# Value products ahead of the next head's scores, w4 in four pieces and a result of four rows, in a decoding attention block

## The chip, the cores and the metric

The kernel runs on one core of a Trainium2 chip. The metric is the device time of one execution in microseconds. A core has engines with queues of their own: TensorE (PE; its weight loads are listed as PEld) multiplies matrices, VectorE (DVE) and ScalarE (ACT) work on elements, GpSimd (POOL) makes a small constant here, and SyncE (SP) issues nearly all loads. Sixteen DMA engines move the data.

## The reference

One token (x, 512 numbers) goes through attention over a cache of 16384 positions and then through a small MLP. There are 32 query heads and 8 key/value heads of 128; four query heads share a key/value head. LN is a layer normalization without weights.

```python
def A(x):                                   # x: LN of the input
    q = (x @ wq) as 32 heads of 128
    scores = q . k_cache * 128 ** -0.5      # 16384 positions, 8 heads of K
    p = softmax(scores)
    return (p . v_cache) @ wo               # 4096 -> 512

def B(x):                                   # x: LN of h
    h = gelu(LN(x) @ w1)
    x1 = x + concat(four shifted quarters of h) @ w2
    return x1 + gelu(LN(x1) @ w3) @ w4      # 512 -> 1792 -> 512

h  = x + A(LN(x))
h2 = h + B(LN(h))
```

With a sequence of one position, each shifted quarter is the padding, that is zero. So the term with w1 and w2 vanishes, x1 is LN(h), and the kernel never loads w1 and w2.

## The kernel before

The kernel is written for each engine as a list of instructions with explicit semaphores (class `Program`). `P.op(engine, ...)` appends an instruction with the tokens that it waits for, and `P.dma("sp", ...)` a load. Each engine works through its list in order, so the order of the calls in the Python text is the order on each engine; engines meet only through tokens. A wait at the head of a list holds back all that stands behind it on that engine.

**Loads.** SP issues all loads but that of x. For a head g these are two halves of K (2 MB each, `kraw`, three buffers), wo(g) (0.5 MB, two buffers), and four pieces of V (1 MB each, six slots: two of their own, `vown`, and four in the place of wq once it has been used, `wq_sb`). A load waits until its buffer has been read: half n of K for the transpose of half n - 3, piece n of V for the products of piece n - 6, wo(g) for project(g - 2). The names k_free, v_free and wo_free hold these tokens. w3 and w4 (1.8 MB each) come last and wait for nothing but their place in SP's list.

**One head.** VectorE transposes K blockwise from `kraw` to `kt`, half by half (`transpose_half`, L226). `scores(g)` (L252) is 128 products on TensorE with kt as weights, `softmax_exp(g)` (L260) four exponentials on ScalarE that also sum up, `denominators(g)` (L266) one fp32 product that adds the sums over partitions, `reciprocal_den(g)` (L284) and `normalize(g)` (L287) two small steps on VectorE. `values(g)` (L276) is 128 products with V as weights, 32 for each piece, and `project(g)` (L296) 16 products with wo that add onto one column of results, `h_ps`. `h_ps` starts with x itself (L305).

**The loop (L309 to L331).** In round g TensorE's list gets scores(g+1), denominators(g), project(g-1), values(g), in this order. VectorE's list gets the two transposes of g+1 with reciprocal_den(g-1) between them, then normalize(g-1). SP's list gets K(g+1), wo(g), V(g). The last round has no K.

**The tail (L332 to L383).** After project(7) two layer normalizations are made in one (L340 to L356), which gives `xc`, the input of the MLP, and `xsum`, all that is added to the MLP's result. Then 56 products with w3 as weights (L366), two Gelus into `hcol` (L370), and 56 products with w4 as weights (L376), whose result is a column layout, 128 partitions by 4; the first waits for all of w4. One add (L381) makes `fin`, and the output is written from 128 partitions, 4 numbers each.

Of the kernel before, what the change touches and what calls it, by code (L numbers as in the profile page):

```python
# [6 lines left out]
FP32 = mybir.dt.float32  # L7
BF16 = mybir.dt.bfloat16
ALU = mybir.AluOpType
# [3 lines left out]
D = 512  # L13
HQ = 32
G = 8
# [4 lines left out]
NCH = D // 128  # L20
NHC = FM // 128
# [4 lines left out]
QTR = NJ * DH  # L26
NKR = 3
NVS = 6
SCALE = 1.0 / math.sqrt(DH)
EPS = 1e-5  # L30

# [50 lines left out]
def bass_sequential_preLN__gqa_block_cached__mixer_s_mlp__decode_kernel(  # L82
# [14 lines left out]
    with ctx:  # L97
        sb = lambda name, shape, dt: ctx.enter_context(nc.sbuf_tensor(name, shape, dt))
        ps = lambda name, shape, dt: ctx.enter_context(nc.psum_tensor(name, shape, dt))
        P = Program(lambda name: ctx.enter_context(nc.semaphore(name)))  # L100
# [7 lines left out]
        xc = sb("xc", [128, NCH], BF16)  # L108
        x1 = sb("x1", [128, NCH], FP32)
        xsum = sb("xsum", [128, NCH], FP32)  # L110
        fin = sb("fin", [128, NCH], BF16)
        mean_f = sb("mean_f", [128, 128], FP32)
        ones_f = sb("ones_f", [128, 128], FP32)
        ident = sb("ident", [128, 128], BF16)
        sel = sb("sel", [128, 4, 128], BF16)
        mask = sb("mask", [128, NQ], FP32)
# [7 lines left out]
        hcol = sb("hcol", [128, NHC], BF16)  # L124
        wo_sb = [sb(f"wo_sb{i}", [128, REP, D], BF16) for i in range(2)]
        w3_sb = sb("w3_sb", [128, NCH, FM], BF16)
        w4_sb = sb("w4_sb", [128, NHC, D], BF16)
# [7 lines left out]
        ot_ps = [ps(f"ot_ps{i}", [128, 512], FP32) for i in range(2)]  # L135
# [6 lines left out]
        w4_in = B_w4.rearrange("(m d) c -> d m c", d=128)  # L142
# [7 lines left out]
        for a in range(NQ):  # L150
            t_mask = P.op("dve", lambda e, a=a: e.memset(mask[32 * a:32 * a + 32, a:a + 1], 1.0), t_m0)
        t_scr = P.op("dve", lambda e: e.memset(scr[:, :], 1.0))
        t_id = P.op("pool", lambda e: e.affine_select(
            out=ident[:, :], in_=ident[:, :], pattern=[[-1, 128]], compare_op=ALU.not_equal,
            fill=1.0, base=0, channel_multiplier=1), t_id0)

        t_sel = None
        for be in range(4):
# [12 lines left out]
        def load_k(g, hf):  # L171
            n = 2 * g + hf
            src = A_k_cache[0, g].rearrange("(p j) d -> p (j d)", p=128)[:, hf * HALF:(hf + 1) * HALF]
            k_land[n] = P.dma("sp", kraw[n % NKR][:, :], src, k_free.get(n - NKR))
# [14 lines left out]
        def stats(src, ln, st, waits, sq_scale=1.0):  # L189
# [9 lines left out]
        t = stats(xcol[:, :], ln1, st1, [t_x])  # L199
        t = P.op("dve", lambda e: e.tensor_scalar(st1[:, 2:3], st1[:, 0:1], st1[:, 0:1], EPS,  # L200
                                                  ALU.mult, ALU.subtract), t)
# [4 lines left out]
        t = P.op("dve", lambda e: e.reciprocal(st1[:, 4:5], st1[:, 3:4]), t)  # L206
# [13 lines left out]
        def transpose_half(g, hf):  # L220
            n = 2 * g + hf
            src = bass.AP(kraw[n % NKR][:, :].bitcast(FP32).tensor, 0,
                          [[HALF // 2, 128], [HALF // 4, 2], [32, 2 * NJ], [1, 32]])
            dst = bass.AP(kt[g % 2][:, :].bitcast(FP32).tensor, 2 * hf,
                          [[HALF, 128], [1, 2], [128, 2 * NJ], [4, 32]])
            k_free[n] = P.op("dve", lambda e: e.transpose(dst, src), k_land[n], t_qk.get(g - 2))  # L226
            return k_free[n]
# [15 lines left out]
        def scores(g):  # L243
            for J in range(NJ):
                for be in range(4):
                    b, e_ = divmod(be, 2)
                    o = J * 512 + b * 256 + e_
                    lhs = bass.AP(kt[g % 2], o, [[2 * HALF, 128], [2, 128]])
                    rhs = Qbd[:, (be * G + g) * 16:(be * G + g + 1) * 16]
                    last = J == NJ - 1 and be == 3  # L250
                    waits = (t_qbd, t_kt[g], t_exp.get(g - 2)) if J == 0 and be == 0 else ()
                    t = P.op("pe", lambda e, J=J, l=lhs, r=rhs, be=be: e.matmul(  # L252
                        s_ps[g % 2][:, 16 * J:16 * J + 16], l, r, start=(be == 0), stop=(be == 3)),
                        *waits, sig=last)
            t_qk[g] = t

        def softmax_exp(g):
            src = s_ps[g % 2][:, :].rearrange("p (t h) -> p h t", h=REP)
            for h in range(REP):
                t_exp[g] = P.op("act", lambda e, h=h: e.activation(  # L260
                    p_sb[g % 2][:, h * 128:(h + 1) * 128], src[:, h, :], ACTF.Exp, scale=float(SCALE),
                    accum_out=accden[g % 2][:, h:h + 1]),
                    *((t_qk[g], t_pv.get(g - 2), t_den.get(g - 2)) if h == 0 else ()), sig=(h == REP - 1))

        def denominators(g):
            t_den[g] = P.op("pe", lambda e: e.matmul(  # L266
                den_ps[:, 0:REP], ones_f[:, :], accden[g % 2][:, :], start=True, stop=True),
                t_exp[g], t_ones, t_rden.get(g - 1))

        def values(g):  # L270
            pv = p_sb[g % 2][:, :].rearrange("p (h t) -> p t h", h=REP)
            for a in range(NQ):
                n = NQ * g + a
                for J in range(NJ):
                    waits = (v_land[n], t_exp[g], t_norm.get(g - 2)) if J == 0 else ()
                    t = P.op("pe", lambda e, J=J, a=a, n=n: e.matmul(  # L276
                        ot_ps[g % 2][:, 0:REP], vslot[n % NVS][:, J * DH:(J + 1) * DH],
                        pv[:, J * NQ + a, :], start=(a == 0 and J == 0),
                        stop=(a == NQ - 1 and J == NJ - 1)), *waits, sig=(J == NJ - 1))
                v_free[n] = t  # L280
            t_pv[g] = t

        def reciprocal_den(g):
            t_rden[g] = P.op("dve", lambda e: e.reciprocal(rden[g % 2][:, :], den_ps[:, 0:REP]), t_den[g])  # L284

        def normalize(g):
            t_norm[g] = P.op("dve", lambda e: e.tensor_tensor(  # L287
                OT[g % 2][:, :], ot_ps[g % 2][:, 0:REP], rden[g % 2][:, :], ALU.mult),
                t_pv[g], t_rden[g], wo_free.get(g - 2))

        def project(g):
            for h in range(REP):
                for k in range(NCH):
                    last = h == REP - 1 and k == NCH - 1
                    lhs = bass.AP(wo_sb[g % 2], h * D + k, [[REP * D, 128], [NCH, 128]])
                    t = P.op("pe", lambda e, h=h, k=k, l=lhs: e.matmul(  # L296
                        h_ps[:, k:k + 1], l, OT[g % 2][:, h:h + 1], start=False,
                        stop=(g == G - 1 and h == REP - 1), skip_group_check=True),
                        *((t_norm[g], wo_land[g]) if h == 0 and k == 0 else ()), sig=last)
            wo_free[g] = t  # L300
# [7 lines left out]
        softmax_exp(0)  # L308
        for g in range(G):  # L309
            if g + 1 < G:  # L310
                for hf in range(2):
                    load_k(g + 1, hf)
                    t_kt[g + 1] = transpose_half(g + 1, hf)
                    if g >= 1 and hf == 0:
                        reciprocal_den(g - 1)
            elif g >= 1:
                reciprocal_den(g - 1)
            load_wo(g)
            for a in range(NQ):
                load_v(g, a)  # L320
                if a == 0:
                    if g >= 1:
                        normalize(g - 1)
                    if g + 1 < G:
                        scores(g + 1)
                        softmax_exp(g + 1)
                    denominators(g)
                    if g >= 1:
                        project(g - 1)
                    pass  # L330
            values(g)  # L331
        t_w3 = P.dma("sp", w3_sb[:, :, :], w3_in)  # L332
        t_w4 = P.dma("sp", w4_sb[:, :, :], w4_in)
        reciprocal_den(G - 1)
        normalize(G - 1)
        project(G - 1)


        P.op("act", lambda e: e.activation(scr[:, 3:4], scr[:, 0:1], ACTF.Sqrt), sig=False)
# [20 lines left out]
        cut = NHC // 2  # L360
        parts = [(0, cut), (cut, NHC)]
        t_h = []
        for i, (m0, m1) in enumerate(parts):
            for m in range(m0, m1):
# [4 lines left out]
                        *((t_xc, t_w3) if m == 0 and k == 0 else ()), sig=(m == m1 - 1 and k == NCH - 1))  # L369
            t_h.append(P.op("act", lambda e, i=i, m0=m0, m1=m1: e.activation(  # L370
                hcol[:, m0:m1], s_ps[i][:, 0:m1 - m0], ACTF.Gelu_apprx_tanh), t))
        for i, (m0, m1) in enumerate(parts):
            for m in range(m0, m1):
                for k in range(NCH):
                    lhs = bass.AP(w4_sb, m * D + k, [[NHC * D, 128], [NCH, 128]])
                    t = P.op("pe", lambda e, m=m, k=k, l=lhs: e.matmul(  # L376
                        ot_ps[0][:, k:k + 1], l, hcol[:, m:m + 1], start=(m == 0 and k == 0),
                        stop=(m == NHC - 1), skip_group_check=True),
                        *((t_h[i], t_w4) if m == m0 and k == 0 else ()),
                        sig=(m == NHC - 1 and k == NCH - 1))  # L380
        t = P.op("dve", lambda e: e.tensor_tensor(fin[:, :], xsum[:, :], ot_ps[0][:, 0:NCH], ALU.add), t, t_sum)  # L381
        t = P.dma("sp", out[0, 0, :].rearrange("(p k) -> p k", k=NCH), fin[:, :], t)
        P.wait("sp", t)  # L383

        block = ctx.enter_context(nc.Block())
# [50 lines left out]
```

## Time and profile before

| | |
|---|---|
| median of three runs | 209.55 us (209.37 to 209.74) |
| the profiled execution | 209.99 us |
| its span (first to last instruction) | 208.1 us |
| DMA: bytes, mean rate | 79.50 MB, 382 GB/s |
| chain that ended last: DMA, DVE, PE, issue | 43%, 25%, 15%, 14% |

The span is 1.9 us shorter than the time of the same execution; the rest lies around it. Rows of the timeline and of the stretches give times in us from the start of the span. In a group's row stand the line, the engine, the operation, what is written and read, the shapes, the count, and after the first bar the busy time and the mean duration of one in ns; after the second bar stands the engine's idle time before them and what ended it. In a row of a stretch stand its bounds and length, the busy time of PE, PEld, DVE, ACT and POOL, the granted clock of TensorE, the busy share of the DMA engines, and GB/s.

### The profile page before, as it was taken

The page shows a single profiled execution, that of the slowest core. Times are in us where ns is not written, and L with a number is a line of the kernel's source. Part 1 is how long each engine was busy: PE and PEld are TensorE (multiplying, and loading weights), DVE is VectorE, ACT ScalarE, POOL GpSimd, SP SyncE. Part 2 cuts the span into 40 slices and gives each one's busy share as a digit, 9 for nine tenths or more (in the row PEclk, how much of TensorE's full clock was granted, in tenths as well). Part 3 has the DMA queues.
Part 4 walks back from the last instruction along what each step waited for, and adds up shares of the span by engine and source line. Part 5 has one row for each costly group of instructions (what it writes and reads, how often), then busy time and mean ns, then how long its engine had stood idle before and what let it go on. Part 6 is the DMA issues. An engine that isn't in the chain of part 4 may idle for free.

```text
span 208.1 us, 5140 instructions
## 1 busy us (share of the span) xinstructions
PE 74.0 (36%) x2441; PEld 72.0 (35%) x2441; DVE 123.4 (59%) x64; ACT 16.1 (8%) x77; POOL 0.5 (0%) x5
## 2 busy tenths in 40 slices
PE   0105115038204730373027500960086107913532
PEld 0005114038204730373027500960086107913432
DVE  2194799963995299519970799069915992100300
ACT  2120002002000200020002000200010000400210
POOL 0000000000000000000000000000000000000000
DMA  6999999999999999999999999999999992699950
GB/s 243 463 403 419 431 422 392 417 431 431 383 416 439 422 389 420 431 422 394 414 436 425 393 415 438 416 404 409 425 441 379 408 402 83 231 411 432 371 175 3
DMA packets 13541, 79.50 MB, mean 382 GB/s; under 512 B 1232, under 2 KB 7120, under 8 KB 7120
## 3 DMA queue, kind: packets, MB, share of 16 engines
q1 hardware_dynamic: 13376, 79.17, 93.1%
q8 instruction: 19, 0.31, 0.6%
q10 hardware_dynamic: 144, 0.00, 0.0%
q14 instruction: 2, 0.02, 0.0%
HBM read 79.17 MB, written 0.00 MB: 380 GB/s over the span
## 4 chain that ended last, share of the span: by engine, by line
DMA 43%; DVE 25%; PE 15%; issue 14%; SPq 1%; ACT 0%
DMA kraw<-in_A_k_cache_dram 29%; DVE kt L226 23%; DMA w_sb<-in_B_w_dram 10%; PE s_ps L252 7%; DMA xcol<-in_A_x_dram 4%; PE ot_ps L276 3%; PE ot_ps L215 2%; SPq L58 1%; PE ot_ps L376 1%; PE den_ps L266 1%; PE h_ps L296 1%; DVE Qbd L238 0%; PE den_ps L193 0%; DVE OT L287 0%; PE ot_ps L234 0%
## 5 line engine op out<-in xcount | busy, mean ns | idle before, releaser
L226 DVE STREAM_TRANSPOSE kt<-kraw 128x4096 f32<-128x4096 f32 x16 | 117.6, 7407 | 40.0 <-DMA kraw<-in_A_k_cache_dram 40.0
L252 PE MATMUL s_ps<-Qbd,kt 128*128 128x16 bf16 x1024 | 28.6, 174 | 87.6 <-DVE OT L287 68.4
L252 PEld LDWEIGHTS s_ps<-Qbd,kt 128*128 128x128 bf16 x1024 | 27.9, 104 | 88.2 <-DVE OT L287 68.9
L276 PE MATMUL ot_ps<-p_sb,wq_sb 128*128 128x4 bf16 x640 | 19.0, 168 | 10.8 <-issue 5.9
L276 PEld LDWEIGHTS ot_ps<-p_sb,wq_sb 128*128 128x128 bf16 x640 | 18.1, 103 | 11.3 <-issue 6.3
L260 ACT ACTIVATE p_sb<-s_ps 128x128 bf16<-128x128 f32 x32 | 8.4, 277 | 157.0 <-PE s_ps L252 157.0
L276 PE MATMUL ot_ps<-p_sb,vown 128*128 128x4 bf16 x384 | 11.6, 168 | 6.6 <-issue 3.7
L276 PEld LDWEIGHTS ot_ps<-p_sb,vown 128*128 128x128 bf16 x384 | 11.1, 104 | 6.9 <-issue 3.8
L287 DVE TENSOR_TENSOR OT<-ot_ps,rden 128x4 bf16<-128x4 f32 x8 | 1.3, 157 | 15.9 <-PE ot_ps L276 15.9
L296 PEld LDWEIGHTS h_ps<-OT,wo_sb 128*128 128x128 bf16 x128 | 6.0, 125 | 2.5 <-issue 2.1
L215 PE MATMUL ot_ps<-xn,wq_sb 128*128 128x1 bf16 x128 | 3.6, 165 | 8.6 <-DVE kt L226 8.6
L260 ACT ACTIVATION_READ_ACCUMULATOR p_sb<-s_ps 128x1 f32 x32 | 6.6, 207 | 0.0
L215 PEld LDWEIGHTS ot_ps<-xn,wq_sb 128*128 128x128 bf16 x128 | 3.5, 104 | 8.7 <-DVE kt L226 8.7
L296 PE MATMUL h_ps<-OT,wo_sb 128*128 128x1 bf16 x128 | 5.5, 172 | 2.3 <-issue 2.1
L266 PE MATMUL den_ps<-accden,ones_f 128*128 128x4 f32 x16 | 4.5, 354 | 0.0
L193 PE MATMUL den_ps<-ln,mean_f 128*128 128x8 f32 x4 | 1.2, 371 | 9.2 <-DVE ln L191 9.2
L193 PEld LDWEIGHTS den_ps<-ln,mean_f 128*128 128x128 f32 x4 | 1.0, 312 | 9.3 <-DVE ln L191 9.3
L381 DVE TENSOR_TENSOR fin<-xsum,ot_ps 128x4 bf16<-128x4 f32 x1 | 0.2, 157 | 6.7 <-PE ot_ps L376 6.7
L266 PEld LDWEIGHTS den_ps<-accden,ones_f 128*128 128x128 f32 x16 | 4.0, 311 | 0.0
L284 DVE RECIPROCAL rden<-den_ps 128x4 f32<-128x4 f32 x8 | 1.3, 163 | 4.4 <-PE den_ps L266 4.4
L190 DVE CAST ln<-xcol 128x4 f32<-128x4 bf16 x1 | 0.2, 171 | 6.0 <-DMA xcol<-in_A_x_dram 6.0
L376 PE MATMUL ot_ps<-hcol,w_sb 128*128 128x1 bf16 x56 | 2.0, 172 | 3.5 <-DMA w_sb<-in_B_w_dram 3.5
(46 smaller groups left out, 19.0 us busy)
## 6 DMA issues: line engine op xcount, KB each, us to landing
kraw<-in_A_k_cache_dram SPq DMA_DIRECT2D x16, 2048.0 KB, 19.6
wq_sb<-in_A_v_cache_dram SPq DMA_DIRECT2D x20, 1024.0 KB, 13.5
vown<-in_A_v_cache_dram SPq DMA_DIRECT2D x12, 1024.0 KB, 13.8
wq_sb<-in_A_wq_dram SPq DMA_DIRECT2D x1, 4096.0 KB, 16.7
wo_sb<-in_A_wo_dram SPq DMA_DIRECT2D x8, 512.0 KB, 8.4
w_sb<-in_B_w_dram SPq DMA_DIRECT2D x2, 1792.0 KB, 19.4
xcol<-in_A_x_dram ACTq DMA_DIRECT2D x1, 1.0 KB, 7.6
out_dram<-fin SPq DMA_DIRECT2D x1, 1.0 KB, 3.1
```

Source lines behind the costliest of these rows:

```text
L58: self.lists[engine].append((waits, lambda e: e.dma_start(out, in_), (sem, 16)))
L193: t = P.op("pe", lambda e: e.matmul(den_ps[:, 0:2 * NCH], mean_f[:, :], ln[:, :], start=True, stop=True), t, t_mean)
L215: t_q = P.op("pe", lambda e, h=h, k=k: e.matmul(ot_ps[0][:, h:h + 1], wq_sb[:, k, h * DH:(h + 1) * DH], xn[:, k:k + 1], start=(k == 0), st ...
L226: k_free[n] = P.op("dve", lambda e: e.transpose(dst, src), k_land[n], t_qk.get(g - 2))
L252: t = P.op("pe", lambda e, J=J, l=lhs, r=rhs, be=be: e.matmul(s_ps[g % 2][:, 16 * J:16 * J + 16], l, r, start=(be == 0), stop=(be == 3)), ...
L260: t_exp[g] = P.op("act", lambda e, h=h: e.activation(p_sb[g % 2][:, h * 128:(h + 1) * 128], src[:, h, :], ACTF.Exp, scale=float(SCALE), ac ...
L266: t_den[g] = P.op("pe", lambda e: e.matmul(den_ps[:, 0:REP], ones_f[:, :], accden[g % 2][:, :], start=True, stop=True), t_exp[g], t_ones, ...
L276: t = P.op("pe", lambda e, J=J, a=a, n=n: e.matmul(ot_ps[g % 2][:, 0:REP], vslot[n % NVS][:, J * DH:(J + 1) * DH], pv[:, J * NQ + a, :], s ...
L284: t_rden[g] = P.op("dve", lambda e: e.reciprocal(rden[g % 2][:, :], den_ps[:, 0:REP]), t_den[g])
L287: t_norm[g] = P.op("dve", lambda e: e.tensor_tensor(OT[g % 2][:, :], ot_ps[g % 2][:, 0:REP], rden[g % 2][:, :], ALU.mult), t_pv[g], t_rden ...
L296: t = P.op("pe", lambda e, h=h, k=k, l=lhs: e.matmul(h_ps[:, k:k + 1], l, OT[g % 2][:, h:h + 1], start=False, stop=(g == G - 1 and h == RE ...
L376: t = P.op("pe", lambda e, m=m, k=k, l=lhs: e.matmul(ot_ps[0][:, k:k + 1], l, hcol[:, m:m + 1], start=(m == 0 and k == 0), stop=(m == NHC ...
```

## The change

It has three parts.

1. The loop is put in another order. SP's list stays as it was. On TensorE a round is now denominators(g), values(g), scores(g+1), project(g); on VectorE both transposes of g+1, reciprocal_den(g), normalize(g). The three steps for head 7 that stood behind the loop are in its last round.
2. w4 is loaded by four DMAs of 5, 4, 3 and 2 of its 14 blocks, each with a semaphore of its own.
3. The products with w4 are turned around. `hcol` (one column) is the weight and 128 columns of w4 are streamed, so the result is four rows of 128, on partitions 0, 32, 64 and 96. `xsum` is brought into the same rows by 16 fp32 products with an identity (`ident_f`, made by VectorE at the start), onto a tile that VectorE has set to zero. The result is copied (128 by 128) to `fin` and written from four partitions, 128 numbers each.

```diff
+W4_CUTS = [(0, 5), (5, 9), (9, 12), (12, 14)]
...
-        fin = sb("fin", [128, NCH], BF16)
+        fin = sb("fin", [128, 128], BF16)
...
+        t_idf = P.op("dve", lambda e: e.tensor_copy(ident_f[:, :], ident[:, :]), t_id)
...
             if g + 1 < G:
-                for hf in range(2):
-                    load_k(g + 1, hf)
-                    t_kt[g + 1] = transpose_half(g + 1, hf)
-                    if g >= 1 and hf == 0:
-                        reciprocal_den(g - 1)
-            elif g >= 1:
-                reciprocal_den(g - 1)
+                load_k(g + 1, 0)
+                load_k(g + 1, 1)
             load_wo(g)
             for a in range(NQ):
                 load_v(g, a)
-                if a == 0:
-                    if g >= 1:
-                        normalize(g - 1)
-                    if g + 1 < G:
-                        scores(g + 1)
-                        softmax_exp(g + 1)
-                    denominators(g)
-                    if g >= 1:
-                        project(g - 1)
-                    pass
+            denominators(g)
+            if g + 1 < G:
+                transpose_half(g + 1, 0)
+                t_kt[g + 1] = transpose_half(g + 1, 1)
+            reciprocal_den(g)
             values(g)
+            normalize(g)
+            if g + 1 < G:
+                scores(g + 1)
+                softmax_exp(g + 1)
+            project(g)
         t_w3 = P.dma("sp", w3_sb[:, :, :], w3_in)
-        t_w4 = P.dma("sp", w4_sb[:, :, :], w4_in)
-        reciprocal_den(G - 1)
-        normalize(G - 1)
-        project(G - 1)
+        t_w4 = [P.dma("sp", w4_sb[:, m0:m1, :], w4_in[:, m0:m1, :]) for m0, m1 in W4_CUTS]
...
-        for i, (m0, m1) in enumerate(parts):
+        t_row = P.op("dve", lambda e: e.memset(ot_ps[0][:, 0:128], 0.0), t_norm[G - 2])
+
+        row_ps = ot_ps[0]
+        for q in range(4):
+            for k in range(NCH):
+                P.op("pe", lambda e, q=q, k=k: e.matmul(
+                    bass.AP(row_ps, 32 * q * 512 + k, [[512, 1], [NCH, 32]]), xsum[:, k:k + 1],
+                    ident_f[:, 32 * q:32 * q + 32], start=(k == 0), stop=False, skip_group_check=True),
+                    *((t_sum, t_idf, t_row) if q == 0 and k == 0 else ()), sig=False)
+        for (m0, m1), t_w in zip(W4_CUTS, t_w4):
             for m in range(m0, m1):
-                for k in range(NCH):
-                    lhs = bass.AP(w4_sb, m * D + k, [[NHC * D, 128], [NCH, 128]])
-                    t = P.op("pe", lambda e, m=m, k=k, l=lhs: e.matmul(
-                        ot_ps[0][:, k:k + 1], l, hcol[:, m:m + 1], start=(m == 0 and k == 0),
-                        stop=(m == NHC - 1), skip_group_check=True),
-                        *((t_h[i], t_w4) if m == m0 and k == 0 else ()),
-                        sig=(m == NHC - 1 and k == NCH - 1))
-        t = P.op("dve", lambda e: e.tensor_tensor(fin[:, :], xsum[:, :], ot_ps[0][:, 0:NCH], ALU.add), t, t_sum)
-        t = P.dma("sp", out[0, 0, :].rearrange("(p k) -> p k", k=NCH), fin[:, :], t)
+                for q in range(4):
+                    waits = (t_w, t_h[int(m >= cut)]) if q == 0 and m in (m0, cut) else ()
+                    t = P.op("pe", lambda e, m=m, q=q: e.matmul(
+                        row_ps[32 * q:32 * q + 1, 0:128], hcol[:, m:m + 1], w4_sb[:, m, 128 * q:128 * (q + 1)],
+                        start=False, stop=(m == NHC - 1), skip_group_check=True),
+                        *waits, sig=(m == NHC - 1 and q == 3))
+        t = P.op("dve", lambda e: e.tensor_copy(fin[:, :], row_ps[:, 0:128]), t)
+        t = P.dma("sp", out[0, 0, :].rearrange("(q c) -> q c", q=4), bass.AP(fin, 0, [[32 * 128, 4], [1, 128]]), t)
```

More of the change, by code (lines that the diff above doesn't have):

```diff
@@ L110, in bass_sequential_preLN__gqa_block_cached__mixer_s_mlp__decode_kernel @@
         xsum = sb("xsum", [128, NCH], FP32)
-        fin = sb("fin", [128, NCH], BF16)
+        fin = sb("fin", [128, 128], BF16)
         mean_f = sb("mean_f", [128, 128], FP32)
         ones_f = sb("ones_f", [128, 128], FP32)
+        ident_f = sb("ident_f", [128, 128], FP32)
         ident = sb("ident", [128, 128], BF16)
```

## The prediction

> **What bounds the kernel now.** I read the page from the top: the engines' shares, the slices, then the queues.
>
> ```profile
> PE 74.0 (36%) x2441; PEld 72.0 (35%) x2441; DVE 123.4 (59%) x64; ACT 16.1 (8%) x77; POOL 0.5 (0%) x5
> GB/s 243 463 403 419 431 422 392 417 431 431 383 416 439 422 389 420 431 422 394 414 436 425 393 415 438 416 404 409 425 441 379 408 402 83 231 411 432 371 175 3
> ...
> q1 hardware_dynamic: 13376, 79.17, 93.1%
> q8 instruction: 19, 0.31, 0.6%
> ```
>
> No engine that computes is above 59%, and the data queue is busy for 93.1% of 16 engines. The kernel is a stream of 79.17 MB. It runs at about 400 GB/s in every slice but the first, the last two, and slices 34 and 35 (83 and 231). Next I asked for the stretches around those two slices.
>
> ```profile
> 20.00:171.00 151.00, 53.53 (x1818) 52.28 (x1815) 109.03 (x28) 8.00 (x56) 0.00 (x0) 1.00 1.01 416
> 171.00:180.00 9.00, 6.97 (x243) 6.97 (x244) 2.16 (x3) 2.63 (x10) 0.00 (x0) 1.00 0.31 110
> 171.00:172.00 1.00, 0.00 (x0) 0.00 (x0) 1.00 (x1) 0.00 (x0) 0.00 (x0) 1.00 0.68 279
> 173.00:174.00 1.00, 0.97 (x36) 0.97 (x37) 0.00 (x0) 0.00 (x0) 0.00 (x0) 1.00 0.39 164
> 174.00:175.00 1.00, 1.00 (x44) 1.00 (x41) 0.00 (x0) 0.00 (x0) 0.00 (x0) 1.00 0.00 0
> 178.00:179.00 1.00, 1.00 (x44) 1.00 (x42) 0.00 (x0) 1.00 (x1) 0.00 (x0) 1.00 0.31 23
> ```
>
> The last two columns are the DMA engines' busy share and GB/s. For 151 us the stream is full at 416 GB/s. From 171 to 180 us it moves 110. From 171 to 174 some of the 16 engines have run out and others (a share of 0.39 in the last of these three) still work; nothing moves at 174, and 0.31 of the engines are back at 178 to 179. The timeline names the cause.
>
> ```profile
> 172.82 0.17 DVE L287 TENSOR_TENSOR OT<-ot_ps,rden 128x4 bf16<-128x4 f32 x1
> 173.03 3.58 PE L252 MATMUL s_ps<-Qbd,kt 128*128 128x16 bf16 x128 [9.23 <-DVE OT L287]
> 176.90 0.67 PE L296 MATMUL h_ps<-OT,wo_sb 128*128 128x1 bf16 x16
> 177.59 0.38 SPq L58 DMA_DIRECT2D wo_sb<-in_A_wo_dram  x1
> 178.01 0.98 SPq L58 DMA_DIRECT2D wq_sb<-in_A_v_cache_dram  x2
> 180.06 0.94 SPq L58 DMA_DIRECT2D w_sb<-in_B_w_dram  x2
> ```
>
> The queue SP issues the load of wo(7) only when project(5) (L296) has read the same buffer. In TensorE's order project(5) stands behind scores(7), and those wait for the last transposes. V(7), w3 and w4 stand behind wo(7) on SP. In earlier heads the same wait is covered by K already queued; for head 7 there is no next K.
>
> The end hangs on that stream:
>
> ```profile
> 192.76 1.02 PE L276 MATMUL ot_ps<-p_sb,vown 128*128 128x4 bf16 x32 [1.48 <-DMA vown<-in_A_v_cache_dram]
> 197.25 1.63 PE L366 MATMUL s_ps<-xc,w_sb 128*128 128x1 bf16 x56 [1.47 <-DVE st L353]
> 198.91 0.18 ACT L370 ACTIVATE hcol<-s_ps 128x7 bf16<-128x7 f32 x1 [0.57 <-PE s_ps L366]
> 202.37 2.00 PE L376 MATMUL ot_ps<-hcol,w_sb 128*128 128x1 bf16 x56 [3.50 <-DMA w_sb<-in_B_w_dram]
> 204.41 0.16 DVE L381 TENSOR_TENSOR fin<-xsum,ot_ps 128x4 bf16<-128x4 f32 x1 [6.74 <-PE ot_ps L376]
> 204.59 0.35 SPq L58 DMA_DIRECT2D out_dram<-fin  x1
> 180.56 21.67 DMA w_sb<-in_B_w_dram
> out_dram<-fin SPq DMA_DIRECT2D x1, 1.0 KB, 3.1
> ```
>
> The last V piece lands at 192.76; hcol is ready at 199.1; w4 lands at 180.56 + 21.67 = 202.2; 56 products, one add and the output follow.
>
> **The change part by part.** *Order in the loop.* TensorE now does den(g), values(g), scores(g+1), project(g); VectorE both transposes of g+1, then the reciprocal and the normalization of g. No instruction is added. SP's order of loads stays; only what it waits for comes earlier. project(5) now follows the products of V(5,3), the load directly ahead of K(7), so wo(7) can be issued most of a head early. V(7,2) and V(7,3) wait for values(6,0) and values(6,1), which run as those pieces land and no longer behind scores(7); w3 and w4 stand behind them without a wait.
>
> The price of the new order is that normalize(g) sits on VectorE ahead of the transposes of g+2, and waits for V(g,3). Loads land in the order of issue, and V(g,3) is issued ahead of K(g+2), so those transposes would be waiting for K anyway. scores(g+1) move behind V(g,3); the transposes must be done by then.
>
> ```profile
> 165.64 7.34 DVE L226 STREAM_TRANSPOSE kt<-kraw 128x4096 f32<-128x4096 f32 x1
> kraw<-in_A_k_cache_dram SPq DMA_DIRECT2D x16, 2048.0 KB, 19.6
> wq_sb<-in_A_v_cache_dram SPq DMA_DIRECT2D x20, 1024.0 KB, 13.5
> ```
>
> For head 7 the transposes end at 165.64 + 7.34 = 173.0, and V(6,3) ends at about 174, so scores(7) start about when they did. K is issued 19.6 and V 13.5 us ahead of landing: that is the cover, and if a wait grew by less than this, nothing would show. Cost of the order within the stream: 0.
>
> What does it bring? If every engine's lost time counts, 9 us x (416 - 110) / 416 = 6.6 us. If only the engines that ran out last count, it is the stretch in which nobody worked, 174.0 to about 178.7 = 4.7 us, since unequal engines stay unequal when no gap lets them draw level. Both ends are from the rows; the 19 instruction fetches of q8 go on beside the data (0.6% of 16 x 208.1 us, some 1 us each) and keep the engines unequal. I take the middle, **-5.7**: V(7,3) lands at 187.1, w3's products end at 198.88 - 5.7 = 193.2, w4 at 196.5.
>
> *w4 in four pieces, the products turned around.* Before, 2.0 us of products wait for all of w4. Now 20, 16 and 12 products can run ahead and only 8 follow the last piece. Each product now streams 128 columns of w4 past one column of hcol. Ahead of them are 16 fp32 products of xsum with the identity. The nearest rows:
>
> ```profile
> L252 PE MATMUL s_ps<-Qbd,kt 128*128 128x16 bf16 x1024 | 28.6, 174 | 87.6 <-DVE OT L287 68.4 <-DVE kt L226 19.2
> L234 PE MATMUL ot_ps<-QT,sel 128*128 128x32 bf16 x4 | 0.3, 194 | 0.3 <-DVE QT L232 0.3
> L366 PE MATMUL s_ps<-xc,w_sb 128*128 128x1 bf16 x56 | 1.6, 165 | 1.5 <-DVE st L353 1.5
> 176.47 0.57 PE L266 MATMUL den_ps<-accden,ones_f 128*128 128x4 f32 x2
> L232 DVE CAST QT<-ot_ps 128x32 bf16<-128x32 f32 x1 | 0.2, 191 | 3.6 <-PE ot_ps L215 3.6
> L238 DVE TENSOR_TENSOR Qbd<-ot_ps,mask 128x512 bf16<-128x512 f32 x1 | 0.7, 690 | 0.4 <-PE ot_ps L234 0.4
> ```
>
> One fp32 product is two instructions (L266: x2, 0.57 us with 128 columns of weights). Bounds for the 16: 32 x 0.028 (L252: 28.6 us / 1024) = 0.9 us, and 16 x 0.57 = 9.1. The weights here are one column, not 128, so I stay near the bottom: 2.0. For a product of 128 columns: 0.028 below; above, (194 - 165) / 31 = 0.94 ns a column, 0.12 us for 128, if each has to end its stream before the next. The four products of one m go to four different groups of rows of the result, and may overlap. I take 0.04, near L234, whose four take (0.3 - 0.19) / 3 = 0.04 apart. So TensorE is at 193.2 + 2.0 + 48 x 0.04 = 197.1 when the last piece (196.5) is there already, and ends 8 x 0.04 later: **197.4** against 204.4, that is -7.0 for both parts, -1.3 of it here. If TensorE were faster, the landing would hold it at 197.0.
>
> [...]
>
> *The result.* The copy of 128x128 replaces an add of 128x4 (0.16). From 0.19 for 32 columns and 0.69 for 512, 128 take 0.29: +0.13. The memset and the identity copy sit where VectorE idles: 0. The output is 4 rows of 256 bytes in place of 128 of 8; landing took 3.1, of which the issue is 0.35. Between nothing and half of the 3.1 saved; no row shows rows of 256 bytes, and most of the 3.1 is the way there and back of any output, so I take -0.4.
>
> Sum: -7.0 + 0.13 - 0.4 = -7.3. The profiled execution took 209.99 us (span 208.1), so 202.7; the median of the runs is 0.44 lower: **202.3**.
>
> **The rivals.** *The turned products run one after another.* 193.2 + 2.0 + 56 x 0.12 = 201.9 at the top of the row, 200.6 at 0.095 each: total 205.4 to 206.8. For it: every stream reads the same 128 partitions. Against: they write different row groups.
>
> *The gap stays, with another releaser.* If the queue still runs dry after V(6,3) because SP waits for products of head 6 that come late (TensorE stalls such as this one would do it),
>
> ```profile
> 158.07 0.40 PE L296 MATMUL h_ps<-OT,wo_sb 128*128 128x1 bf16 x8 [2.06 <-issue]
> ```
>
> then only the tail is won: 209.55 - 1.3 - 0.3 = 208.0. Against: behind V(6,0) stand three more pieces of V(6), wo(7) and two of V(7) before V(7,2) has its turn, 5.8 MB or 13 us at 416 GB/s. One such stall between V(7,3) and hcol costs up to 2 us of 3.1 us of slack (199.1 to 202.2); it is in the range.
>
> *Slower.* The fp32 products and the turned ones both cost their upper end: 9.1 + 6.7 = 15.8, so TensorE ends at 209.0 in place of 204.4, total 213.9. It decides from 11.5 us of TensorE work after w3's products on; I count 4.2.
>
> **How the numbers follow.** Forecast (200.5 to 203.8): 0.68. Products one after another, 203.8 to 207: 0.18. Gap stays: 0.07. Slower: 0.03. Another small gain: 0.04. Below: the stream wins 6.6, the output 0.8 and TensorE waits for the landing: 200.6. The range that holds 8 in 10 reaches into the first rival: 200.5 to 205.5. A measurement of this kernel can tell about 0.2% from no change: faster 0.95, same 0.01, slower 0.04.
>
> **What would show it.** Right: no slice below 370 GB/s between the second and the one in which w4 ends; wo(7) issued long before 170 us; w4's last piece at 195.6 to 197.5; 8 products after it. Wrong: a gap after V(6,3); TensorE still busy with products over 1 us after the last piece; identity products over 3 us; transposes that wait for normalize and no longer for K.

## The result and the profile after

| | before | changed |
|---|---|---|
| median, us | 209.65 (209.37 to 209.93, 4 runs) | 197.94 (197.86 to 198.07, 4 runs) |
| span of the profiled execution, us | 208.1 | 196.1 |
| changed / before | | 0.944, 95% interval 0.943 to 0.946 |

The gain is 11.7 us. The prediction said 7.3, and its range began at 200.5, so the measured time lies below it. The sign and the order of the parts were right; the size was not.

The page of the changed kernel first: the slices and the queue of loads.

```profile
GB/s 211 438 428 428 434 428 404 423 436 428 405 430 428 438 425 409 428 439 431 389 428 439 438 392 430 429 438 413 413 428 441 424 409 424 411 423 428 419 280 28
...
q1 hardware_dynamic: 13288, 79.17, 97.0%
```

The hole of two slices is gone, and the queue is busy for 97.0% of the span. But the slices also look higher than before. Two stretches of the changed kernel, and the first of them in the kernel before:

```profile
20.00:160.00 140.00, 57.99 (x1842) 54.98 (x1839) 101.61 (x28) 7.99 (x56) 0.00 (x0) 1.00 1.01 424
171.00:180.00 9.00, 7.31 (x242) 7.14 (x242) 0.34 (x2) 2.63 (x10) 0.00 (x0) 1.00 1.03 426
```
```profile
20.00:160.00 140.00, 51.51 (x1753) 50.41 (x1751) 98.03 (x26) 8.00 (x56) 0.00 (x0) 1.00 1.01 417
```

In both kernels the busy share of the DMA engines is 1.01 there, so both streams are full, yet one moves 424 GB/s and the other 417. Nothing in the prediction makes a full stream faster. The end of the changed kernel, from the chain and the timeline:

```profile
184.46 1.02 PE L279 MATMUL ot_ps<-p_sb,vown 128*128 128x4 bf16 x32 [1.41 <-DMA vown<-in_A_v_cache_dram]
190.53 0.18 ACT L365 ACTIVATE hcol<-s_ps 128x7 bf16<-128x7 f32 x1 [0.52 <-PE s_ps L361]
185.89 7.42 DMA w_sb<-in_B_w_dram
193.35 0.34 PE L380 MATMUL ot_ps<-w_sb,hcol 128*1 128x128 bf16 x8 [0.15 <-DMA w_sb<-in_B_w_dram]
193.75 0.29 DVE L384 CAST fin<-ot_ps 128x128 bf16<-128x128 f32 x1 [4.21 <-PE ot_ps L380]
194.07 0.64 SPq L59 DMA_DIRECT2D out_dram<-fin  x1
```

Set beside the lines of before, the 12.0 us between the spans come out in four terms:

| | before | changed | gain, us |
|---|---|---|---|
| w4 has landed (180.56 + 21.67; 185.89 + 7.42) | 202.2 | 193.3 | 8.9 |
| from there to the last step on VectorE | 2.2 | 0.44 | 1.7 |
| that step, its start to the issue of the output | 0.18 | 0.32 | -0.14 |
| from the issue of the output to the end of the span | 3.5 | 2.0 | 1.5 |

The prediction had 5.7, 1.3, -0.13 and 0.4. So the largest error stands in the first row: the stream ends 3.2 us earlier than the closed hole explains.

### The profile page after: what moved, and what is told of

It is laid out like the page before. It is cut to its first block, busy times and chain, and to the rows that moved or that the text cites. A ratio compares the mean times of both kernels' runs of the same rounds, so it can differ in the third digit from the quotient of the medians.

```text
span 196.1 us, 5207 instructions
## 1 busy us (share of the span) xinstructions
PE 78.8 (40%) x2473; PEld 74.0 (38%) x2473; DVE 124.7 (64%) x66; ACT 16.1 (8%) x77; POOL 0.5 (0%) x5
## 4 chain that ended last, share of the span: by engine, by line
DMA 77%; SPq 11%; DVE 8%; PE 2%; issue 1%; ACT 0%
DMA vown<-in_A_v_cache_dram 34%; DMA wq_sb<-in_A_v_cache_dram 24%; DMA kraw<-in_A_k_cache_dram 12%; SPq L59 11%; DVE kt L229 7%; DMA xcol<-in_A_x_dram 4%; DMA w_sb<-in_B_w_dram 4%; PE ot_ps L279 1%; PE den_ps L196 0%; PE ot_ps L380 0%; ACT st L206 0%; DVE fin L384 0%; DVE xn L210 0%; DVE st L203 0%; DVE ln L193 0%
## 5 line engine op out<-in xcount | busy, mean ns | idle before, releaser
L279 PE MATMUL ot_ps<-p_sb,wq_sb 128*128 128x4 bf16 x640 | 20.1, 169 | 49.1 <-DMA wq_sb<-in_A_v_cache_dram 49.1
L279 PEld LDWEIGHTS ot_ps<-p_sb,wq_sb 128*128 128x128 bf16 x640 | 18.7, 104 | 50.6 <-DMA wq_sb<-in_A_v_cache_dram 50.6
L279 PE MATMUL ot_ps<-p_sb,vown 128*128 128x4 bf16 x384 | 12.2, 169 | 27.5 <-DMA vown<-in_A_v_cache_dram 27.5
L299 PEld LDWEIGHTS h_ps<-OT,wo_sb 128*128 128x128 bf16 x128 | 5.0, 117 | 2.2 <-issue 1.9
```

Of the source, the lines that this page charges most:

```text
L279: t = P.op("pe", lambda e, J=J, a=a, n=n: e.matmul(ot_ps[g % 2][:, 0:REP], vslot[n % NVS][:, J * DH:(J + 1) * DH], pv[:, J * NQ + a, :], s ...
L299: t = P.op("pe", lambda e, h=h, k=k, l=lhs: e.matmul(h_ps[:, k:k + 1], l, OT[g % 2][:, h:h + 1], start=False, stop=(g == G - 1 and h == RE ...
```

## The experiments

**Two theories for the faster stream.** Theory A, place: the change made `fin` larger and added `ident_f`. Tiles are laid out one behind the other in each partition, so everything behind them moved. In the compiled programs the first buffer that is loaded behind them, wo_sb0, starts at byte 22560 before (88 x 256 + 32) and at 23296 after (91 x 256); all other buffers of the stream stand at multiples of 4096 or 2048 from it, so all start 32 bytes past a multiple of 256 before, and on one after. Theory B, order: loads are issued earlier, and a longer queue runs faster. The kernels ran in three sessions of four, each on one chip with the kernel before run beside them. The first four take the change apart.

**The place alone.**

```diff
         fin = sb("fin", [128, NCH], BF16)
+        pad = sb("pad", [128, 112], BF16)
```

> The kernel before with an unused tile of 224 bytes behind fin, so that every buffer that a load fills starts at a multiple of 256 bytes in its partition (before: 32 bytes past one; after the change: at a multiple, because fin and ident_f grew). Nothing else differs. Theory A, place: the whole stream runs faster wherever the buffers start on 256, at 424 GB/s instead of 416 from 20 to 160 us, a piece of V comes every 2.45 us and not 2.50, and the end comes 3 to 4 us earlier: 205.6 to 206.8 us, with the gap after V(6,3) still there. Theory B, order: the faster stream comes from loads being issued earlier; then this kernel takes 209.4 to 209.9 and streams at 416.

Measured: 208.57 us against 211.92 for the kernel before in the same session, ratio 0.985 (0.983 to 0.987), that is -3.35 us. The gain is the expected one, while the expected time of 205.6 to 206.8 was missed: the kernel before was slower in the later sessions than the 209.65 above, most of it probably by its output (below). An unused tile of 224 bytes has brought 3.3 us. The stretch:

```profile
20.00:160.00 140.00, 53.45 (x1819) 52.29 (x1817) 100.47 (x26) 7.98 (x56) 0.00 (x0) 1.00 1.01 424
171.00:180.00 9.00, 8.44 (x282) 8.35 (x278) 0.52 (x3) 2.63 (x10) 0.00 (x0) 1.00 0.46 155
```

The stream runs at 424 with the loop of before, and the hole is still there (155 GB/s). Theory A holds.

**The place taken back from the changed kernel.**

```diff
         fin = sb("fin", [128, 128], BF16)
+        pad = sb("pad", [128, 16], BF16)
```

> The changed kernel with an unused tile of 32 bytes behind fin, so that the buffers of the loads start 32 bytes past a multiple of 256, as before the change. Theory A, place: the stream falls back to 416 GB/s and the time rises by 3 to 4 us to 201.0 to 202.0. Theory B, order: 197.8 to 198.1, at 424 GB/s.

Measured: 201.85 us, 3.8 more than the changed kernel (198.05 in the next session), at 417 GB/s:

```profile
20.00:160.00 140.00, 56.67 (x1820) 53.83 (x1818) 98.82 (x28) 6.84 (x48) 0.00 (x0) 1.00 1.01 417
```

**How much place.** Two more kernels put the buffers of the changed kernel elsewhere, with unused tiles of 128 and of 256 bytes in that line.

> The changed kernel with an unused tile of 128 bytes behind fin, so that the buffers of the loads start 128 bytes past a multiple of 256. If it is multiples of 256 that count, the stream falls to 416 GB/s (a V piece every 2.49 us) and the whole is 3.5 to 4 us slower than the changed kernel, as with 32 bytes. If multiples of 64 or 128 are enough, no difference (424 GB/s, 2.45 us).

> The changed kernel with an unused tile of 256 bytes, so that the loads' buffers start at a multiple of 512 (in the changed kernel 256 past one). If 256 is all that counts: 197.9 to 198.2, a V piece every 2.45 us. If more is gained at 512: below 197.6.

Measured: 201.04 us at 128 bytes past a multiple (3.0 us slower than the changed kernel on the same chip, less than the 3.5 to 4 expected), and 198.08 us on multiples of 512 (no difference from the changed kernel's 197.94 and 198.05). The stretch at 128 past, then on 512:

```profile
20.00:160.00 140.00, 57.44 (x1847) 54.60 (x1843) 99.11 (x28) 7.20 (x51) 0.00 (x0) 1.00 1.01 418
```
```profile
20.00:160.00 140.00, 58.07 (x1845) 55.05 (x1841) 101.62 (x28) 7.98 (x56) 0.00 (x0) 1.00 1.01 424
```

So of the places tried, those on multiples of 256 are fast; 128 past is not enough, though a little less bad than 32, and 512 brings nothing more. The single packets say the same. Worked out from the packets that the traces keep, a packet of 8 KB took 317 ns in the mean between 20 and 160 us in each of the four kernels at 32 past (before, the changed one moved there, the order alone below, the tail alone below), 316 at 128 past, and 310 in every kernel on 256 or 512.

**The order alone.** The loop of the change, with w4 in one DMA, the old tail, the old output, and every buffer where it was.

```diff
             denominators(g)
+            if g + 1 < G:
+                transpose_half(g + 1, 0)
+                t_kt[g + 1] = transpose_half(g + 1, 1)
+            reciprocal_den(g)
             values(g)
+            normalize(g)
+            if g + 1 < G:
+                scores(g + 1)
+                softmax_exp(g + 1)
+            project(g)
```

> The kernel before with the new order of the loop alone; w4 in one piece, the old products, the old output, and every buffer where it was before. Theory A: the gap goes and the rate stays at 416 GB/s; gain 5.0 to 5.8 us, 203.9 to 204.7. Theory B: the rate rises to 424 too, gain 8.5 to 9.5, 200.2 to 201.2.

Measured: 206.26 us against 211.92, -5.7 us. The rate stays at 417, and the hole is closed:

```profile
20.00:160.00 140.00, 57.20 (x1838) 54.35 (x1836) 98.86 (x28) 7.06 (x50) 0.00 (x0) 1.00 1.01 417
171.00:180.00 9.00, 5.64 (x198) 5.47 (x199) 2.31 (x3) 0.00 (x0) 0.00 (x0) 1.00 1.03 407
```

In this trace w4 has landed at 197.2 instead of 202.2 (171.82 + 25.34), 5.1 us earlier. The absolute time expected (203.9 to 204.7) was missed because the kernel before was slower by 2.3 us beside these four. Theory B falls: the loads are issued early (wo(7) at 160.28 and no longer at 177.59), and the rate does not rise.

**Order and place together.** The kernel of the order alone with the unused tile of 224 bytes.

> The kernel before with the new order of the loop and the loads' buffers on multiples of 256 (an unused tile of 224 bytes), with the old tail and the old output. If the order and the place add up, it is the kernel of the order alone less 3.3 to 3.8 us: 202.4 to 203.0 on a chip where before takes 211.7 to 211.9. If the place helps only because the loads of the old order queue late, it adds less than 2 us.

Measured: 202.41 us against 211.51, -9.1 us; 5.7 and 3.35 add up to 9.0. The landing of w4, which the output cannot touch, tells the same. The load's rows for the place alone, the order alone and both:

```profile
177.97 20.94 DMA w_sb<-in_B_w_dram
```
```profile
171.82 25.34 DMA w_sb<-in_B_w_dram
```
```profile
169.27 24.16 DMA w_sb<-in_B_w_dram
```

It lands at 198.9, 197.2 and 193.4 in place of 202.2: 3.3, 5.1 and 8.8 us earlier. So the two parts add up, within 0.4 us.

**The tail alone.** The loop of before with the changed tail; `fin` and `ident_f` stand behind the loads' buffers, and a small tile keeps fin's old place.

```diff
-        fin = sb("fin", [128, NCH], BF16)
+        spare = sb("spare", [128, NCH], BF16)
...
         vown = [sb(f"vown{i}", [128, QTR], BF16) for i in range(NVS - NCH)]
+        fin = sb("fin", [128, 128], BF16)
+        ident_f = sb("ident_f", [128, 128], FP32)
```

> The loop of before with the changed tail alone (w4 in four pieces, the turned products, four rows written), and every buffer of the loads where it was before (fin and ident_f stand at the end of the memory). By the two traces the wait from w4's landing to the last step on VectorE shrinks from 2.2 to 0.45 us (-1.7), the copy costs +0.13, and from the issue of the output to the end 3.5 us become 2.0 (-1.5): 206.4 to 206.8. By the prediction's own terms (-1.3, +0.13, -0.4) it would be 208.0. If the shorter output in the profile belongs to the emptier end of that run alone, 207.8 to 208.1.

Measured: 207.02 us (0.2 above the expected range) against 211.92, -4.9 us, more than the 3.0 read from the two first traces. Its last lines:

```profile
202.32 0.04 issue
202.37 0.41 PE ot_ps L389 x5
202.78 0.02 issue
202.80 0.29 DVE fin L393
```

w4 lands at 202.3, as in the trace of before, and the step on VectorE follows 0.48 us behind it. The rest is the output, issued at 203.12 in a span of 205.2 us: 2.1 us, while the two kernels run beside it that have the old output took 4.9 (201.28 to 206.2, the place alone) and 5.1 (199.52 to 204.6, the order alone).

**The output alone.** To see whether that belongs to the output itself, the changed kernel was run beside a copy that writes from 128 partitions again (what it writes is not the result).

```diff
-        t = P.dma("sp", out[0, 0, :].rearrange("(q c) -> q c", q=4), bass.AP(fin, 0, [[32 * 128, 4], [1, 128]]), t)
+        t = P.dma("sp", out[0, 0, :].rearrange("(p k) -> p k", k=NCH), fin[:, 0:NCH], t)
```

> The changed kernel as it is, beside the next three on one chip. The kernel before was 2.3 us slower in the session of the first four runs than when the change was timed, and the runs of that session with the old output took 4.9 to 5.1 us from the issue of the output to the end of the span, not 3.5. If that is the old output alone, the changed kernel keeps 197.8 to 198.2 even where before takes 211.9; if the chip is slower all over, it takes 200.1.

> The changed kernel, but the output is written as before, from 128 partitions with 4 numbers each (the first 4 columns of fin, so the numbers written aren't the result). Theory O: the many short rows take the time; from the issue of the output to the end of the span 3.5 to 5.1 us in place of 2.0, and the whole is 1.5 to 3.1 us slower than the changed kernel on this chip. Prediction's term: 0.4 slower. Rival, that the output's time follows what the queue did before it: no difference.

Measured: 198.05 us for the changed kernel in a session where before took 211.69, so the chip was not slower all over; and 201.41 with the old output, +3.4 us, a little more than the 1.5 to 3.1 expected. The issues of DMAs of the old output in that copy, and of the kernel with the place alone:

```profile
out_dram<-fin SPq DMA_DIRECT2D x1, 1.0 KB, 5.1
```
```profile
out_dram<-fin SPq DMA_DIRECT2D x1, 1.0 KB, 4.5
```

The old output takes 3.1 us to landing in the first trace of before, and 4.5, 4.7, 5.1 and 4.5 in the four later traces that have it. The new one leaves 2.0 or 2.1 us from issue to the end of the span in every trace that has it. So in the three later sessions the old output landed 1.4 to 2.0 us later than in the first trace, and the kernel before took 1.9 to 2.3 us longer than at first (211.51 to 211.92 against 209.65). Before itself was not traced again in those sessions, so that the one is the cause of the other is an inference. Why the old output took longer there stays open.

**w4 in one DMA.** The changed kernel with `W4_CUTS = [(0, 14)]`.

> The changed kernel with w4 in one DMA. All else as changed: the turned products, the four rows. w4 lands when the last piece landed (193.3 us in the trace), and then come all 56 products: at the measured 0.04 us each 2.2 us, to the last step on VectorE 2.4 us after the landing and not 0.45, so 1.9 us slower than the changed kernel: 199.8 to 200.0. Rival: the four products of a block overlap so well that most of this is gone, 198.5; or one DMA lands earlier than four, by up to 0.3.

Measured: 199.23 us, +1.2 on the changed kernel of the session before (198.05; the kernel on multiples of 512 beside it took 198.08), less than expected. The chain:

```profile
169.03 24.27 DMA w_sb<-in_B_w_dram
193.30 0.04 issue
193.34 1.69 PE ot_ps L380 x56
```

All of w4 lands at 193.3, as its last piece did. The 56 products take 1.69 us, 0.030 each, not 0.04: where four pieces arrive, TensorE's pace is partly that of the landings (in the changed kernel it sits idle 1.2 us in all, four times, until a piece has landed).

**What is left: engines that lag.** The prediction left it open whether the closed hole would bring 4.7 or 6.6 us, since, by its argument, instruction fetches keep the DMA engines unequal. Every second value product was left out, which takes 1024 instructions from TensorE.

```diff
-                for J in range(NJ):
+                for J in range(0, NJ, 2):
```

> The changed kernel with every second value product left out (16 of 32 for each piece of V), so that TensorE has 1024 instructions fewer and the queue of instruction fetches about 4 packets fewer (15 in place of 19). TensorE isn't what the end waits for in either. Theory F: each fetch of 16 KB holds one DMA engine up by about 1.4 us and the engine that is hit most often sets the end, so the last piece of w4 lands 1.2 to 1.6 us earlier: 196.4 to 196.8. Rival: the fetches cost only their share of all 16 engines, 4 x 1 us / 16 = 0.25 us: 197.6 to 197.8.

Measured: 196.75 us, -1.3 on the changed kernel of the session before (198.05) and on the kernel on multiples of 512 beside it (198.08). The page's row of the instruction queue and the last stretches, for this kernel:

```profile
q8 instruction: 15, 0.25, 0.4%
...
190.00:191.00 1.00, 1.00 (x42) 0.91 (x31) 0.00 (x0) 0.00 (x0) 0.00 (x0) 1.00 0.48 166
191.00:192.00 1.00, 0.69 (x17) 0.20 (x12) 0.00 (x0) 0.00 (x0) 0.00 (x0) 1.00 0.24 83
192.00:193.00 1.00, 0.38 (x8) 0.10 (x8) 0.29 (x1) 0.00 (x0) 0.00 (x0) 1.00 0.00 0
```

and for the changed kernel:

```profile
q8 instruction: 19, 0.31, 0.6%
...
190.00:191.00 1.00, 1.00 (x41) 0.99 (x40) 0.00 (x0) 0.19 (x2) 0.00 (x0) 1.00 0.54 193
191.00:192.00 1.00, 1.00 (x53) 1.00 (x47) 0.00 (x0) 0.00 (x0) 0.00 (x0) 1.00 0.39 132
192.00:193.00 1.00, 0.83 (x28) 0.45 (x18) 0.00 (x0) 0.00 (x0) 0.00 (x0) 1.00 0.13 44
```

In the changed kernel only about half of the engines still work between 190 and 191 us (0.54), and the work of about two is left between 192 and 193 (0.13 of 16). With 4 fetches fewer the last are done a microsecond earlier (w4's last piece lands at 192.1 in place of 193.3). A share of all 16 engines would be 0.25 us, so that rival falls, and the time is the one that theory F gave: the end waits for the engines that were held up most.

The kernel changes more than the number of fetches, but the packets that the traces keep add to it. The 1.4 us of theory F are there: in the changed kernel a fetch took 0.88 to 0.97 us, and with 17 of the 19 a data packet that began just before the fetch ended took 0.47 to 0.55 us longer than the usual one of its size, 1.4 us together. The fetches took 921, 961, 967, 948, 886, 886, 936 and 931 ns, then 924, 964, 969, 948, 879, 879, 935 and 931, and so on: the lengths repeat after eight, as if the fetches went round eight of the engines in turn. Then 19 fetches leave eight engines with none, five with two and three with three, while 15 leave none with three. This fits the two stretches: half of the engines done first in both, and in the changed kernel two or three that go on for over a microsecond behind the others. A trace does not name the engine of a packet, so the turn is an inference.

**A try to beat the changed kernel.** w4 dealt out so that each partition reads one run.

```diff
-        w4_in = B_w4.rearrange("(m d) c -> d m c", d=128)
+        w4_in = B_w4.rearrange("(d m) c -> d m c", d=128)
...
-                        s_ps[i][:, m - m0:m - m0 + 1], w3_sb[:, k, 128 * m:128 * (m + 1)], xc[:, k:k + 1],
+                        s_ps[i][:, m - m0:m - m0 + 1], bass.AP(w3_sb, k * FM + m, [[NCH * FM, 128], [NHC, 128]]), xc[:, k:k + 1],
```

> The changed kernel with w4's rows dealt out differently: partition d holds rows 14 d to 14 d + 13, so that a piece is one run of 2 to 5 KB in each partition and not rows of 1 KB; the products with w3 take every 14th column to match. Theory: a row of 1 KB costs 46 to 48 ns and a run less per KB, so w4 takes 0.2 to 0.4 us less and the end, which waits for its last piece, comes as much earlier; the weights in steps of 14 cost the products with w3 about 0.5 us (36 in place of 28 ns, as for steps of 4), which the wait for w4 covers. 197.5 to 197.8 where the changed kernel takes 197.9. Rival: the end is set by the engines that lag, and the runs bring nothing.

Measured: 199.38 us, 1.3 slower than the changed kernel beside it. The chain shows why:

```profile
189.15 3.50 PE s_ps L361 x56
192.65 0.93 PE ot_ps L372 x26
193.58 1.67 PE ot_ps L380 x55
```

Weights taken in steps of 14 cost 3.50 / 56 = 63 ns a product, not the expected 36, so TensorE became the bound. The longer runs did not pay either: the last data packet of the stream ends at 192.96 us in this trace and at 192.99 in that of the changed kernel beside it. No version that beats the changed kernel and computes all of the reference came out of these runs.

## Why the prediction was wrong in size

**What bounds the kernel, and the hole: right.** The page was read correctly: a full stream with one hole, made by wo(7) behind project(5). In the changed kernel wo(7) is issued at 158.20, V(7,2), V(7,3), w3 and w4 follow from 165.5 on, and 171 to 180 us moves 426 GB/s.

```profile
158.20 0.38 SPq L59 DMA_DIRECT2D wo_sb<-in_A_wo_dram  x1
```

Of the signs that were named, wo(7) and the 8 last products came out. w4's last piece, at 193.3, came earlier than 195.6 to 197.5, and the last slice but one (280) is below 370 not by a wait but because half of the engines are done (a share of 0.54 between 190 and 191 us).

**The hole's size: near.** 5.7 was taken between 4.7 and 6.6. The order alone brought 5.1 in its trace and 5.7 by the times. That the middle agrees with the times is in part luck: it was chosen as a middle, not worked out. The lower end was argued from unequal engines, and those were seen at the end of the changed kernel (shares of 0.54, 0.39 and 0.13 in its three rows above).

**The step that failed** is the one that priced the new tiles: "The memset and the identity copy sit where VectorE idles: 0", together with "Cost of the order within the stream: 0" and the rate of 416 GB/s, which was carried over to the changed kernel. The copy is indeed free as an instruction: 0.21 us of VectorE at 1.7 us of the span, ahead of 6.0 us in which it sits idle until x lands. But `ident_f` and the larger `fin` move every buffer behind them in memory, and with it the stream that bounds the kernel: 3.35 us alone on the kernel before, 3.8 us when taken from the changed one. No term stood for it, and no rival; the range could not reach it. The sum with 3.3 us for it would have been 199.0. What is left, 1.1 us, is as much as the output was taken too small by; the misses of the hole and of the tail go against each other.

**The products: right in kind.** They overlap: 0.04 us each was assumed, 0.030 were measured where all of w4 was there (56 in 1.69 us, w4 in one DMA), while a single one is listed with 0.31 us (the median of L380 in the changed kernel). The fp32 products cost 1.0 to 1.2 us (L372 there, 190.4 to 191.3 by the starts), not 2.0. So TensorE was not the last, the landing was (the prediction's 197.0 case), and the tail gained 1.7 rather than 1.3. The first rival, products one after another, falls: its 0.12 us each would make 6.7 us of the 56, where 1.69 were measured. Two small slips of the prediction's working changed nothing: no row gives the rival's lower price of 0.095 us a product, and the 5.8 MB behind V(6,0) are 14 us at 416 GB/s, not 13.

**The output: mis-sized.** -0.4 was taken between 0 and half of 3.1, because most of the 3.1 was thought to be the way of any output. It was -1.5 in the two traces compared, and -3.4 by the times in a later session: the whole of the new output, from issue to the end of the span, is 2.0. The 3.1 of the one trace was the lowest of five.

**The rivals** "the gap stays" and "slower" did not occur: no hole is left, and TensorE's last products ended 0.4 us behind the landing.

## What to carry to other kernels

When a kernel is bound by loads, list what a change does to the addresses of the loaded buffers, as one lists its instructions: here a tile that no load touches was worth 3.3 us, because the buffers behind it came to stand on multiples of 256 bytes. Before crediting a new order with a faster stream, run the old order with the new addresses. A term that rests on one duration of one trace, as the output did, deserves both ends in the range.

## What was not expected of the hardware

- A full stream into buffers 32 bytes past a multiple of 256 runs at 417 GB/s, 128 past at 418, on multiples of 256 or 512 at 424, with the DMA share at 1.01 each time. What was moved here is the side that is written; by what mechanism its place counts, no run shows.
- An output of 128 rows of 8 bytes took 3.1 to 5.1 us to land and left 3.5 to 5.5 us from issue to the end of the span; four rows of 256 bytes leave 2.0 to 2.1.
- Instruction fetches stand among the packets of the DMA engines (q8: 19 of 16 KB, 0.88 to 0.97 us each in the changed kernel), and their number goes with TensorE's instructions: with 1024 fewer there were 15, and w4's last piece landed 1.2 us earlier (192.1 in place of 193.3).
- Weights read in steps of 14 elements cost 63 ns a product (L361 with w4 in runs: 3.50 / 56), in steps of 4 36 ns (L376 before: 2.00 / 56), without steps 29 (L366 before: 1.63 / 56).
